# Turning two more x tiles in halves on two engines, and reordering the first products of v, in a fused attention and gated-MLP kernel

## The chip, the cores and the metric

The kernel runs on one core of a Trainium2 chip. The metric is the device time of one execution in microseconds (us), lower is better.

## The reference, cut to what matters

```python
xn = _layernorm(x)                              # x: 1 x 2048 x 512, bfloat16
return x + A(xn, wqkv, w_phi, wo) + B(xn, w_gate, w_up, w_down)
# A: qkv = xn @ wqkv; softmax features of q and k (32 heads of 16); kv = phi_k^T v; o = phi_q kv / den; o @ wo
# B: ((xn @ w_gate) * (xn @ w_up)) @ w_down     # 512 -> 1792 -> 512
```

Only the start matters here. Before TensorE can do useful work, the first four row tiles of x (128 x 512 each) must be loaded, have their row means removed ("centring"), and be transposed on TensorE ("turned"), since the products take it in that form. The division by the standard deviation is applied later, so it does not hold up the start. The product v(t) of a tile is four matmuls, one for each K-block of 128 rows of the v weights.

## The kernel before

TensorE's order is fixed by the program (`sc.pin = True`); every step waits by semaphore for what it reads. ScalarE is `act`, VectorE is `dve`.

```python
    load_x(0, 1)                 # loads, in the order of issue; SP and ACT are the two issuing queues
    load_x(1, 1, ACT)
    load_v(SP, 0)
    load_v(ACT, 1)
    load_x(2, 1)
    load_v(ACT, 3)
    load_v(SP, 2)
    load_x(3, 1)
    load_gu(SP, 0, (1,))         # first up weights
    ...
    load_gu(ACT, 0, (0,))        # first gate weights
```

```python
    def ln_mean_split(t):        # half the row mean on each of ScalarE and VectorE
        act(xn_tile(t)[:, 256:], x_tile(t)[:, 256:], ..., accum=mu[:, t:t + 1])
        dve(... xn_tile(t)[:, :256] ... accum_out=mua[:, t:t + 1] ...)
    def ln_mean(t):              # the whole mean on ScalarE
        act(xn_tile(t), x_tile(t), [("x", t)], [("mu", t)], scale=1.0 / 512.0, accum=mu[:, t:t + 1])
    def x_transpose(t, b, h=0, parts=1, eng=ACT):
        # 4 // parts transposes of 128x128 into PSUM bank b, then one copy ("turn") to SBUF by eng
```

```python
    x_transpose(0, 2, 0, 2)      # tiles 0 and 1: in halves; tile 1's copies on VectorE
    x_transpose(0, 3, 1, 2)
    warm(1, 128)
    x_transpose(1, 4, 0, 2, DVE)
    x_transpose(1, 5, 1, 2, DVE)
    warm(1, 128)
    ln_mean_split(2)
    ln_center_whole(2)
    ln_mean(3)
    ln_center(3)
    v_matmul(0, 0, (0,))         # K-blocks 0, 1 of v for tiles 0 and 1
    v_matmul(1, 1, (0,))
    v_matmul(0, 0, (1,))         # K-blocks 2, 3
    v_matmul(1, 1, (1,))
    x_transpose(2, 6)            # tile 2: whole, one copy on ScalarE
    for t in range(ND):
        ln_moments(t)            # row statistics, VectorE
    ...
    g0a()                        # first half of the first gate unit
    x_transpose(3, 7)            # tile 3: whole, one copy on ScalarE
    v_matmul(2, 2)
    v_keep(2, 2)
    u0a()                        # first half of the first up unit
    v_matmul(3, 3)
    v_keep(3, 3)
    g1a()                        # "the third gate group"
    ...
    w_fold(1, 0, 2)              # later: the first weight fold, used below as a mark
```

The eight `warm` matmuls of 512 columns ahead of this piece work on constants; they keep TensorE busy while the first loads are under way.

## Time and profile before

| | before |
|---|---|
| time, median of 3 runs (lowest, highest) | 214.45 us (214.41, 214.79) |
| span of the profiled execution | 212.6 us |
| TensorE busy | 207.7 us, 98% |
| x tile 3 landed | 7.26 us |
| first weight fold starts | 15.27 us |

The page of the kernel before: busy time by engine, and the chain of work that ended last.

```profile
span 212.6 us, 4025 instructions
...
PE 207.7 (98%) x1455; PEld 125.2 (59%) x1476; DVE 166.5 (78%) x277; ACT 144.6 (68%) x350; POOL 109.8 (52%) x137
...
PE 94%; DMA 2%; SPq 1%; issue 1%; DVE 0%; ACT 0%; DVEq 0%
```

TensorE (PE) is the bound. But the end of a matmul in this profile is modelled and overlaps the next one's start, so busy time hides short waits. The way to see them is the distance from one start to the next: it is 216, 109 or 56 ns for 512, 256 or 128 columns when nothing holds TensorE up, and anything above is a late start. One exception: a hole of exactly one more matmul (as the 432 ns, twice 216, before the start at 56.03 us in the kernel before) is taken for a record that the trace lacks, since other profiles have none at that place. The Trainium skill, "TensorE: Matmul & The Clock Gate", section "Wait — 56ns, not 53.3ns?", gives N / 2.4 GHz + 2.5 ns, which is 215.8 and 55.8 ns; this trace agrees.

The same chain in order of time, its first stretch: start, length, and what the time went to.

```profile
...
2.65 4.61 DMA arena<-in_A_x_dram
7.28 0.73 ACT arena L228 x2
8.11 0.36 DVE arena L451
8.52 0.40 PE ps L485 x4
8.92 1.95 PE ps L247 x11
10.87 0.05 issue
10.92 4.51 PE ps L247 x32
```

The load of x tile 3 lands at 7.26 us (2.65 + 4.61), ScalarE takes its mean (two instructions), VectorE centres it (L451), and only then do the transposes of tile 3 (L485) start, at 8.52. From there on TensorE waits no more.

### The profile page before, as it was taken

The page shows a single profiled execution, that of the slowest core. Times are in us where ns is not written, and L with a number is a line of the kernel's source. Part 1 is how long each engine was busy: PE and PEld are TensorE (multiplying, and loading weights), DVE is VectorE, ACT ScalarE, POOL GpSimd, SP SyncE. Part 2 cuts the span into 40 slices and gives each one's busy share as a digit, 9 for nine tenths or more (in the row PEclk, how much of TensorE's full clock was granted, in tenths as well). Part 3 has the DMA queues.
Part 4 walks back from the last instruction along what each step waited for, and adds up shares of the span by engine and source line. Part 5 has one row for each costly group of instructions (what it writes and reads, how often), then busy time and mean ns, then how long its engine had stood idle before and what let it go on. Part 6 is the DMA issues. An engine that isn't in the chain of part 4 may idle for free.

```text
span 212.6 us, 4025 instructions
## 1 busy us (share of the span) xinstructions
PE 207.7 (98%) x1455; PEld 125.2 (59%) x1476; DVE 166.5 (78%) x277; ACT 144.6 (68%) x350; POOL 109.8 (52%) x137
## 2 busy tenths in 40 slices
PE   8999999999999999999999999999999999999995
PEld 2575444444554444444444444556888898899884
DVE  4659999987995547568699988986888898898622
ACT  5588899985889999978778967564544444432220
POOL 4032464540330366998995882004559559558540
PEclk9999999999999999999999999999999999999999
DMA  5999990699100230331611340414265736637411
GB/s 172 299 300 376 162 175 6 80 343 196 25 3 0 35 63 3 52 67 33 88 40 23 71 80 0 119 53 51 49 79 125 172 78 152 141 85 175 123 49 49
DMA packets 49251, 22.29 MB, mean 105 GB/s; under 512 B 38096, under 2 KB 47696, under 8 KB 49232
## 3 DMA queue, kind: packets, MB, share of 16 engines
q1 hardware_dynamic: 48272, 21.39, 45.4%
q10 hardware_dynamic: 960, 0.66, 1.0%
q8 instruction: 11, 0.18, 0.4%
q14 instruction: 8, 0.07, 0.1%
HBM read 11.03 MB, written 2.10 MB: 62 GB/s over the span
## 4 chain that ended last, share of the span: by engine, by line
PE 94%; DMA 2%; SPq 1%; issue 1%; DVE 0%; ACT 0%; DVEq 0%
PE ps L247 89%; DMA arena<-in_A_x_dram 2%; PE ps L563 2%; PE ps L621 2%; PE ps L381 1%; SPq L292 0%; SPq L272 0%; ACT arena L228 0%; DVE arena L934 0%; PE ps L485 0%; DVE arena L451 0%; DVEq L1359 0%
## 5 line engine op out<-in xcount | busy, mean ns | idle before, releaser
L247 PE MATMUL ps<-arena 128*128 128x512 bf16 (+2 forms) x1139 | 197.8, 329 | 1.1
L247 PEld LDWEIGHTS ps<-arena 128*128 128x128 bf16 (+1 forms) x1160 | 110.6, 98 | 73.6 <-ACT arena L228 0.5
L228 ACT ACTIVATE arena<-ps 128x512 bf16<-128x512 f32 (+4 forms) x117 | 59.2, 541 | 11.2 <-PE ps L247 7.9
L228 ACT ACTIVATE arena<-arena 128x32 f32<-128x32 f32 (+9 forms) x131 | 53.1, 421 | 11.4 <-DVE arena L517 6.0
L904 DVE TENSOR_TENSOR arena<-ps,arena 128x512 f16<-128x512 f32 (+1 forms) x56 | 38.3, 683 | 13.3 <-PE ps L247 7.0
L527 POOL TENSOR_TENSOR arena<-arena 128x1024 bf16<-128x1024 bf16 x16 | 31.8, 1993 | 26.7 <-ACT arena L228 26.7
L517 DVE TENSOR_REDUCE arena<-arena 128x64 f32<-128x1024 bf16 x32 | 38.2, 1212 | 8.1 <-ACT arena L228 7.9
L228 ACT ACTIVATE arena<-ps,arena 128x512 bf16<-128x512 f32 (+1 forms) x55 | 35.6, 663 | 11.4 <-PE ps L247 11.0
L865 POOL TENSOR_TENSOR arena<-arena 128x256 f16<-128x256 f16 x32 | 23.8, 755 | 14.3 <-DMA arena<-arena 13.1
L843 DVE TENSOR_TENSOR arena<-arena 128x896 f16<-128x896 f16 x32 | 26.0, 811 | 3.4 <-PE ps L247 3.4
L228 ACT ACTIVATE ps<-ps 128x256 f32<-128x256 f32 x24 | 8.8, 368 | 29.0 <-PE ps L247 20.9
L934 DVE SCALAR_TENSOR_TENSOR arena<-ps,arena 128x256 bf16<-128x256 f32 (+1 forms) x24 | 13.2, 566 | 8.9 <-PE ps L247 8.8
L783 POOL TENSOR_TENSOR arena<-arena 128x512 f16<-128x512 bf16 x14 | 16.3, 1173 | 6.1 <-DVE arena L904 5.2
L969 POOL TENSOR_TENSOR arena<-arena 128x512 f32<-128x512 f32 x8 | 9.5, 1191 | 17.0 <-ACT arena L228 17.0
L533 POOL TENSOR_TENSOR arena<-arena 128x512 bf16<-128x512 bf16 x16 | 16.9, 1058 | 0.8
L631 DVE TENSOR_TENSOR arena<-ps,arena 128x512 f16<-128x512 f32 x16 | 11.0, 685 | 1.3 <-ACT arena L228 0.5
L531 POOL TENSOR_TENSOR arena<-arena 128x32 f32<-128x32 f32 x16 | 5.2, 324 | 10.4 <-ACT arena L228 5.9
L405 DVE BATCH_NORM_STATS2 arena<-arena 128x6 f32<-128x512 bf16 x16 | 10.4, 670 | 0.0
L463 POOL TENSOR_SCALAR arena<-arena 128x1 f32<-128x1 f32 x12 | 3.1, 274 | 12.9 <-ACT arena L228 12.9
L678 DVE BATCH_NORM_STATS2 arena<-arena 128x6 f32<-128x512 bf16 x14 | 8.9, 680 | 0.0
L563 PEld LDWEIGHTS ps<-arena 128*128 128x128 bf16 x128 | 6.1, 97 | 3.5
L621 PEld LDWEIGHTS ps<-arena 128*128 128x128 bf16 x128 | 6.2, 97 | 1.2
(55 smaller groups left out, 70.5 us busy)
## 6 DMA issues: line engine op xcount, KB each, us to landing
arena<-in_A_x_dram SPq DMA_DIRECT2D x8, 256.0 KB, 3.3
out_dram<-arena SPq DMA_DIRECT2D x15, 128.0 KB, 2.0
arena<-in_B_w_down_dram SPq DMA_DIRECT2D x1, 1792.0 KB, 9.1
arena<-in_A_x_dram SPq DMA_DIRECT2D x3, 512.0 KB, 4.3
arena<-arena SPq DMA_TRANSPOSE x44, 3.1
arena<-in_B_w_gate_dram SPq DMA_DIRECT2D x1, 640.0 KB, 8.5
arena<-in_B_w_up_dram SPq DMA_DIRECT2D x1, 640.0 KB, 9.6
arena<-in_B_w_gate_dram SPq DMA_DIRECT2D x1, 512.0 KB, 5.0
```

The source lines that it names most:

```text
L228: return sc.step(ACT, lambda e: e.activation(out=out_ap, in_=in_ap, func=func, scale=scale, **kw), reads, writes, 130.0 + 0.833 * n)
L247: ins = e.matmul(out_ap, lhsT=l, rhs=r, start=start and i == 0, stop=stop and i == npair - 1, **kw)
L517: dve(lambda e: e.tensor_reduce(out=sm, in_=e_v, axis=AX.X, op=ALU.add), [(name, s, 0), (name, s, 1)], [("sums", sr)], 1024)
L527: pool(lambda e: e.tensor_tensor(out=e_w, in0=e_w, in1=r_w, op=ALU.mult), [(name, s, 0), (name, s, 1), ("rs", n)], [(name, s, 0), (name, s ...
L533: pool(lambda e: e.tensor_tensor(out=e_v[:, :, 1, :], in0=e_v[:, :, 1, :], in1=rat[:, :, None].to_broadcast([128, H, 16]), op=ALU.mult), [ ...
L621: ins = e.matmul(bank(b0 + c // 4, (c % 4) * CW, CW), lhsT=ph[:, c, :], rhs=kvz_v[:, c, :], start=True, stop=True)
L631: dve(lambda e: e.tensor_tensor(out=o_tile(t).rearrange("p (b h f) -> p b h f", b=2, f=16), in0=nd[:, :, :, 0:16], in1=w_v[:, r].unsqueeze ...
L783: pool(lambda e, ft=ft: e.tensor_tensor(out=hH_v[:, ft, 0:512], in0=hT_v[:, ft, 0:512], in1=r2w, op=ALU.mult), [("hT", ft, 0), "r2w", ("x" ...
L843: dve(lambda e, k=k, i0=i0, i1=i1, op=op: e.tensor_tensor(out=s_block(p, k), in0=i0, in1=i1, op=op), ks + more, [s_key(p, k)] + over.get(k ...
L865: pool(lambda e, k=k, i0=i0, i1=i1, op=op: e.tensor_tensor(out=so_block(p, k), in0=i0, in1=i1, op=op), ks + [("so", p, m) for m in more], ...
L904: dve(lambda e: e.tensor_tensor(out=h_v[:, ft, sg * 512:(sg + 1) * 512], in0=bank(bu), in1=g, op=ALU.mult), [("ps", bu), ("g", s)] + ([("j ...
L934: dve(lambda e: e.scalar_tensor_tensor(out=o, in0=src, scalar=inv, in1=resid, op0=ALU.mult, op1=ALU.add), keys + [rkey, "inv"], [("ostg", ...
```

## The change

Its intent: give VectorE half of the turns of tiles 2 and 3 and half of the mean of tile 3, and put matmuls whose inputs are there ahead of those that wait. K-block 3 of v, loaded ahead of block 2, is used ahead of it; v(2) goes ahead of the first gate unit and of the transposes of tile 3.

```diff
+    x_transpose(0, 2, 0)
+    x_transpose(0, 3, 1)
     warm(1, 128)
+    x_transpose(1, 4, 0, DVE)
+    ln_mean_split(2)
+    x_transpose(1, 5, 1, DVE)
     warm(1, 128)
-    ln_mean_split(2)
     ln_center_whole(2)
-    ln_mean(3)
-    ln_center(3)
-    v_matmul(0, 0, (0,))
-    v_matmul(1, 1, (0,))
-    v_matmul(0, 0, (1,))
-    v_matmul(1, 1, (1,))
-    x_transpose(2, 6)
+    for t in range(2):
+        v_matmul(t, t, ((0, 1),), stop=False)
+    for t in range(2):
+        v_matmul(t, t, ((3,),), start=False, stop=False)
+    x_transpose(2, 6, 0)
+    x_transpose(2, 4, 1, DVE)
+    for t in range(2):
+        v_matmul(t, t, ((2,),), start=False)
+    ln_mean_split(3)
+    ln_center_whole(3)
+    (g0a, u0a, g0b, u0b), gate0 = up_unit(*ups.pop(0), pairs, 2)
+    (g1a, u1a, g1b, u1b), gate1 = up_unit(*ups.pop(0), pairs, 2)
+    v_matmul(2, 2)
+    x_transpose(3, 7, 0)
+    x_transpose(3, 6, 1, DVE)
+    v_keep(2, 2)
     for t in range(ND):
         ln_moments(t)
     ...
     g0a()
-    x_transpose(3, 7)
-    v_matmul(2, 2)
-    v_keep(2, 2)
     u0a()
```

(Helper functions lose the whole-tile case.)

More of the change, by code (lines that the diff above doesn't have):

```diff
@@ L401, in xk @@
     def xk(t):
-        return [("xnT", t, 0), ("xnT", t, 1)] if t < 2 else [("xnT", t)]
+        return [("xnT", t, 0), ("xnT", t, 1)] if t < ND else [("xnT", t)]
     def ln_moments(t):
@@ L441, in ln_center_whole @@
             [("x", t), ("mua", t), ("mu", t)], [("xn", t, 0)], 512, 0.27)
-    def ln_mean(t):
-        act(xn_tile(t), x_tile(t), [("x", t)], [("mu", t)], scale=1.0 / 512.0, accum=mu[:, t:t + 1])
-    def ln_center(t, parts=1):
-        n = 512 // parts
-        m, k = (mv_v[:, t, 0:1], ("mv", t)) if t % 2 == 0 else (mu[:, t:t + 1], ("mu", t))
-        for h in range(parts):
-            hs = slice(h * n, (h + 1) * n)
-            dve(lambda e, hs=hs: e.tensor_scalar(out=xn_tile(t)[:, hs], in0=x_tile(t)[:, hs], scalar1=m, scalar2=None,
-                                                 op0=ALU.subtract), [("x", t), k], [("xn", t, h)], n, 0.27)
     def ln_deferred():
@@ L475, in x_turn, with x_transpose @@
                turn=True)
-    def x_transpose(t, b, h=0, parts=1, eng=ACT):
-        n = NQ // parts
+    def x_transpose(t, b, h, eng=ACT):
+        n = NQ // 2
         qs = slice(h * n, (h + 1) * n)
@@ L486, in fn @@
             return ins
-        sc.step(PE, fn, [("xn", t, h), "ident"], [("ps", b)], n * 60.0)
+        sc.step(PE, fn, [("xn", t, h if t < 2 else 0), "ident"], [("ps", b)], n * 60.0)
         o = sb("xnT", 0, NQ * S_TOK).rearrange("p (q s) -> p q s", q=NQ)[:, qs, t * 128:(t + 1) * 128]
         i = bank16(b, 0, n * 128).rearrange("p (q s) -> p q s", q=n)
-        w = [("xnT", t, h)] if parts == 2 else [("xnT", t)]
+        w = [("xnT", t, h)]
         if eng == ACT:
@@ L538, in vs_tile, with v_matmul @@
         return sb("vs", (t % RK) * H * HC, H * HC).rearrange("p (h c) -> p h c", h=H)
-    def v_matmul(t, b, hs=(0, 1)):
-        for h in hs:
-            mm(bank(b), [(xnT(q, t * 128, 128), wv_v[:, q, :]) for q in (2 * h, 2 * h + 1)],
-               ([("xnT", t, h)] if t < 2 else [("xnT", t)]) + [("wv", 2 * h), ("wv", 2 * h + 1)], b, start=h == 0, stop=h == 1)
+    def v_matmul(t, b, qs=((0, 1), (2, 3)), start=True, stop=True):
+        for n, part in enumerate(qs):
+            mm(bank(b), [(xnT(q, t * 128, 128), wv_v[:, q, :]) for q in part],
+               ([("xnT", t, part[0] // 2)] if t < ND else [("xnT", t)]) + [("wv", q) for q in part], b,
+               start=start and n == 0, stop=stop and n == len(qs) - 1)
     def v_keep(t, b):
@@ L1022, in _build @@
     ln_center_split(1)
-    x_transpose(0, 2, 0, 2)
-    x_transpose(0, 3, 1, 2)
+    x_transpose(0, 2, 0)
+    x_transpose(0, 3, 1)
     warm(1, 128)
-    x_transpose(1, 4, 0, 2, DVE)
-    x_transpose(1, 5, 1, 2, DVE)
+    x_transpose(1, 4, 0, DVE)
+    ln_mean_split(2)
+    x_transpose(1, 5, 1, DVE)
     warm(1, 128)
-    ln_mean_split(2)
     ln_center_whole(2)
-    ln_mean(3)
-    ln_center(3)
-    v_matmul(0, 0, (0,))
-    v_matmul(1, 1, (0,))
-    v_matmul(0, 0, (1,))
-    v_matmul(1, 1, (1,))
-    x_transpose(2, 6)
+    for t in range(2):
[14 more added lines that the diff above has]
+    v_keep(2, 2)
     for t in range(ND):
         ln_moments(t)
-    (g0a, u0a, g0b, u0b), gate0 = up_unit(*ups.pop(0), pairs, 2)
-    (g1a, u1a, g1b, u1b), gate1 = up_unit(*ups.pop(0), pairs, 2)
     g0a()
-    x_transpose(3, 7)
-    v_matmul(2, 2)
-    v_keep(2, 2)
     u0a()
```

## The prediction

> **What bounds the kernel.** TensorE: the busy table gives it 207.7 of 212.6 us (98%), and the chain that ended last is 94% TensorE. In the timeline, matmul by matmul, starts follow each other every 216, 109 or 56 ns (512, 256, 128 columns). The Trainium skill, "TensorE: Matmul & The Clock Gate", "Wait — 56ns, not 53.3ns?", gives N / 2.4 GHz + 2.5 ns; the trace agrees. After 8.52 us no start is late, apart from holes of exactly one matmul (192 to 216 ns), which I take for missing records. So the change can only win before 8.52 us. From 5.49 us (first v product) on there are three real gaps: 0.17 us at 6.53 (third K-block of v, landed 6.43), 0.13 at 7.74 (first gate weights, landed 7.69), 0.33 at 8.52 (centring of tile 3, done 8.46). Sum 0.63 us, 0.3% of the time: the ceiling.
>
> **What the change does.** Same matrix work, another order; two more turns on VectorE, one more half mean.
> 1. K-block 3 of v (landed 5.60) goes ahead of block 2, which now follows the transposes of tile 2: removes the 0.17 us.
> 2. v(2) (4 x 0.216 us) goes ahead of the gate unit, so the gate starts near 8.7 us, after its weights: removes the 0.13 us.
> 3. Turns of tiles 2 and 3 split: a whole turn on ScalarE took 0.58 to 0.60 us, halves 0.38 (ScalarE) and 0.29 (VectorE) in parallel. v(2) needs this: only 0.43 us of products cover it.
> 4. Mean of tile 3 split: 0.42 + 0.19 us on ScalarE for 0.63 + 0.19 (0.1 to 0.2 less), but ScalarE first turns half of tile 2 (7.10 to 7.48), so the mean starts at about 7.40, not 7.28. Centring ends at about 8.42, hardly before 8.46, but v(2) now covers it instead of the short gate unit.
>
> **Estimate from those durations.** Block 3 of both tiles 6.35 to 6.79; transposes of tile 2 to 7.01; block 2 to 7.44; v(2) waits about 0.10 us for ScalarE's half turn and runs 7.54 to 8.40; transposes of tile 3 wait about 0.08 us; gate unit at 8.70; v(3) at 9.57, no wait; third gate group at 10.44, against 10.90 by summed cadences. Gain 0.45 us.
>
> **Afterwards.** All of it is on the critical path and should last, if nobody else becomes late. VectorE starts the row statistics at about 9.07, not 8.38, so rstd comes about 0.7 us later. By my count ScalarE has caught up by 18 us, 0.3 us before the first k features.
>
> **Prediction.** 214.45 - 0.45 = 214.0 us; 8 in 10: 213.7 to 214.45. Faster by over 2%: 0.01; within 2%: 0.98; slower: 0.01.
>
> **What the profile would show.** (1) no gap before block 3, none on a DMA before block 2; (2) no wait on gate weights; (3) v(2) starts at 7.5 to 7.6, released by ScalarE or VectorE; (4) transposes of tile 3 at 8.4 to 8.6, released by the centring; third gate group at about 10.45; no start late between 9 and 139 us; span about 212.15.
>
> **What would make it wrong.** Loads landing 0.2 us later or in another order; the half turns slower on both engines at once than alone; the VectorE order (copy, mean, copy, centring) delaying tile 2's centring beyond 6.7; late rstd stalling the first folds or features, which could give back all of it; a variation between runs (0.38 us here) as large as the gain.

## The result, and the profile after

| | before | after |
|---|---|---|
| time, median of 6 runs (lowest, highest) | 214.60 us (214.41, 214.85) | 214.44 us (213.88, 215.03) |
| ratio of means, 95% interval | | 0.9989 (0.9969 to 1.001) |
| span of the profiled execution | 212.6 us | 212.9 us |
| x tile 3 landed | 7.26 us | 7.41 us |
| first weight fold starts | 15.27 us | 15.15 us |
| late starts of TensorE from 50 to 62 us | none | 0.38 us |

A ratio is the mean time of one kernel's fast runs over the mean of the other's of the same rounds, so it is not quite the ratio of the medians in the table. The median lies in the forecast range, at its very upper end. The gain is 0.16 us by the medians and 0.23 by the means, a third to a half of what was forecast, but the interval reaches from about 0.7 us faster to 0.2 slower: these times alone rule out neither the forecast gain nor none. The profiled execution after is even longer than the one before. The times of the changed kernel spread over 1.15 us here, those of the kernel before over 0.44; that is no property of the kernels, since later the kernel before spread over 0.98 to 1.33 us (11 executions each).

The page of the changed kernel: the lines that answer to those of before.

```profile
span 212.9 us, 4028 instructions
...
PE 208.2 (98%) x1455; PEld 125.3 (59%) x1476; DVE 167.3 (79%) x281; ACT 143.8 (68%) x350; POOL 109.9 (52%) x137
...
PE 96%; DMA 1%; DVE 1%; issue 1%
```

Its chain in order of time, from the start.

```profile
...
0.79 2.60 DMA arena<-in_A_x_dram
3.41 0.56 DVE arena L427 x3
...
4.49 0.65 PE ps L474 x4
5.14 0.11 PE ps L1001
5.25 0.43 PE ps L474 x4
5.68 0.11 PE ps L1001
5.78 1.55 PE ps L247 x6
7.33 0.22 PE ps L474 x4
7.56 1.40 PE ps L247 x6
8.96 0.28 PE ps L474 x4
9.23 1.52 PE ps L247 x11
```

L427 are half means, L474 transposes, L1001 a warming matmul, L247 the products. The chain no longer goes through the load of tile 3. It starts with tile 0 (landed 3.39) and runs through TensorE from 4.49 us on. That was the aim. But the same matmuls now take longer than they should. First, the first product of v, before and then after, as the timeline shows it (start, duration).

```profile
5.49 0.38 PE L247 MATMUL ps<-arena 128*128 128x512 bf16 x1
```

```profile
5.58 0.63 PE L247 MATMUL ps<-arena 128*128 128x512 bf16 x1
```

0.63 us for a matmul that took 0.38: in the execution after, TensorE was still at half its rate. Start to start it took 427 ns, then 303 (part at half, part at full rate), then 216. Full rate came at about 5.3 us in the execution before and at about 6.2 in the one after. Up to 5.47 us both programs give TensorE the same instructions, so the change can hardly have caused this; the same program, run again below, reached full rate at about 5.65 us. The two late starts that came of it, 0.21 and 0.09 us, and some slow transposes ahead of them took most of the gain of the front.

Second, the stretch from 50 to 62 us. VectorE in the kernel before, two groups of its timeline, with the idle time ahead of them in brackets:

```profile
50.38 0.41 DVE L465 TENSOR_SCALAR arena<-arena 128x512 bf16<-128x512 bf16 x1 [1.36 <-DMA arena<-arena]
...
53.94 0.68 DVE L904 TENSOR_TENSOR arena<-ps,arena 128x512 bf16<-128x512 f32 x1
```

In the changed kernel, with TensorE's weight loads (PEld) that had to wait:

```profile
51.11 0.41 DVE L454 TENSOR_SCALAR arena<-arena 128x512 bf16<-128x512 bf16 x1 [2.20 <-DMA arena<-arena]
...
54.67 0.68 DVE L894 TENSOR_TENSOR arena<-ps,arena 128x512 bf16<-128x512 f32 x1
...
55.41 0.55 PEld L247 LDWEIGHTS ps<-arena 128*128 128x128 bf16 x4 [0.46 <-DVE arena L894]
...
58.37 0.55 PEld L247 LDWEIGHTS ps<-arena 128*128 128x128 bf16 x4 [0.47 <-DVE arena L894]
...
60.23 0.23 PEld L381 LDWEIGHTS ps<-arena 128*128 128x128 bf16 x4 [0.43 <-ACT arena L228]
```

VectorE normalises a later x tile (L465, L454) into a buffer that a transposing DMA must have read first. That DMA was 0.73 us later, so everything behind it in VectorE's queue was too, also the gate product (L904, L894) that frees a PSUM bank for TensorE. Three matmul starts, at 55.41, 58.38 and 60.24 us, were 0.13, 0.14 and 0.10 us late. The first two waited for that gate product, the third for ScalarE (L228), which had itself waited for VectorE until 54.79 us, again 0.73 later than in the kernel before. The busy time of the stretch doesn't show it, as the windows view of before and after says (columns: stretch, its length, then busy time of TensorE and so on):

```profile
50.00:62.00 12.00, 11.95 (x72) 5.86 (x72) 11.62 (x19) 8.92 (x21) 1.93 (x1) 1.00 0.24 47
```

```profile
50.00:62.00 12.00, 11.95 (x68) 5.28 (x67) 10.89 (x18) 8.09 (x18) 1.93 (x1) 1.00 0.28 56
```

TensorE is busy 11.95 of 12 us in both, with 0.38 us of late starts and without.

The transposing DMAs stand in SP's queue behind the loads of w_down and, right after it, wo. The DMA view of before and after (count, size, us from issue to landing):

```profile
arena<-in_B_w_down_dram SPq DMA_DIRECT2D x1, 1792.0 KB, 9.1
```

```profile
arena<-in_B_w_down_dram SPq DMA_DIRECT2D x1, 1792.0 KB, 10.1
```

It was issued 0.1 us earlier in the changed kernel (39.08, not 39.19) and still landed 0.85 us later. The load of wo behind it landed 0.72 us later (50.52, not 49.80), and the first transposing DMA behind both 0.73 later (51.01, not 50.28). In all eleven profiles that keep the two loads in this place, that DMA landed 0.47 to 0.56 us after the load of wo. So "slow w_down load" below stands for the two loads together.

### The profile page after: what moved, and what is told of

It is laid out like the page before. It is cut to its first block, busy times and chain, and to the rows that moved or that the text cites. A ratio compares the mean times of both kernels' runs of the same rounds, so it can differ in the third digit from the quotient of the medians.

```text
span 212.9 us, 4028 instructions
## 1 busy us (share of the span) xinstructions
PE 208.2 (98%) x1455; PEld 125.3 (59%) x1476; DVE 167.3 (79%) x281; ACT 143.8 (68%) x350; POOL 109.9 (52%) x137
## 4 chain that ended last, share of the span: by engine, by line
PE 96%; DMA 1%; DVE 1%; issue 1%
PE ps L247 91%; PE ps L611 2%; PE ps L553 2%; DMA arena<-in_A_x_dram 1%; PE ps L381 1%; PE ps L474 1%; DVE arena L427 0%; DVE arena L924 0%; DVE arena L434 0%; PE ps L1001 0%
## 5 line engine op out<-in xcount | busy, mean ns | idle before, releaser
L247 PE MATMUL ps<-arena 128*128 128x512 bf16 (+2 forms) x1139 | 198.4, 329 | 1.1
L247 PEld LDWEIGHTS ps<-arena 128*128 128x128 bf16 (+1 forms) x1160 | 110.7, 98 | 73.8 <-ACT arena L228 1.2
L228 ACT ACTIVATE arena<-ps 128x512 bf16<-128x512 f32 (+3 forms) x117 | 58.6, 539 | 12.9 <-PE ps L247 7.0
L228 ACT ACTIVATE arena<-arena 128x32 f32<-128x32 f32 (+9 forms) x131 | 52.9, 423 | 11.3 <-DVE arena L506 7.2
L894 DVE TENSOR_TENSOR arena<-ps,arena 128x512 f16<-128x512 f32 (+1 forms) x56 | 38.2, 683 | 11.8 <-PE ps L247 6.1
L228 ACT ACTIVATE arena<-ps,arena 128x512 bf16<-128x512 f32 (+1 forms) x55 | 35.9, 672 | 10.9 <-PE ps L247 10.4
L228 ACT ACTIVATE ps<-ps 128x256 f32<-128x256 f32 x24 | 8.8, 368 | 29.0 <-PE ps L247 27.0
L553 PEld LDWEIGHTS ps<-arena 128*128 128x128 bf16 x128 | 6.1, 97 | 3.5
L454 DVE TENSOR_SCALAR arena<-arena 128x512 bf16<-128x512 bf16 x12 | 5.4, 484 | 2.8 <-DMA arena<-arena 2.6
## 6 DMA issues: line engine op xcount, KB each, us to landing
arena<-in_B_w_down_dram SPq DMA_DIRECT2D x1, 1792.0 KB, 10.1
```

Source lines behind the costliest of these rows:

```text
L228: return sc.step(ACT, lambda e: e.activation(out=out_ap, in_=in_ap, func=func, scale=scale, **kw), reads, writes, 130.0 + 0.833 * n)
L247: ins = e.matmul(out_ap, lhsT=l, rhs=r, start=start and i == 0, stop=stop and i == npair - 1, **kw)
L894: dve(lambda e: e.tensor_tensor(out=h_v[:, ft, sg * 512:(sg + 1) * 512], in0=bank(bu), in1=g, op=ALU.mult), [("ps", bu), ("g", s)] + ([("j ...
```

## The experiments

**Theory 1.** The change works as forecast on the front, but two things that differ between executions of one program hid it in this profile: when TensorE's clock steps up, and how long loads take. The kernel before absorbs a late clock in its waits; the changed kernel has no waits left to absorb it. **Theory 2.** The change itself, by its later row statistics, causes the stall at 50 us.

Three columns below are read from traces. "Landing" is that of x tile 3; "fold" the start of the first weight fold, which all work of the front precedes; "late 50-62" the sum of late matmul starts in that stretch. Each kernel has 6 executions (one of them profiled). The means are of those. Runs 1 to 4, 5 to 8 and 9 to 12 in the table, without its first two rows, ran on three chips. Differences are taken from the nanoseconds of the trace.

| run | mean us | before | ratio, 95% interval | landing | fold | fold - landing | w_down load | late 50-62 |
|---|---|---|---|---|---|---|---|---|
| before (profile) | | | | 7.26 | 15.27 | 8.00 | 9.1 | 0 |
| after (first result) | 214.39 | 214.62 | 0.9989, 0.9969 to 1.001 | 7.41 | 15.15 | 7.74 | 10.1 | 0.38 |
| before_again | 214.71 | 214.71 | 1.0001, 0.9983 to 1.0019 | 7.53 | 15.54 | 8.00 | 9.0 | 0 |
| after_again | 214.31 | 214.71 | 0.9981, 0.9963 to 0.9999 | 7.57 | 15.01 | 7.45 | 8.2 | 0 |
| before_wd_early | 214.72 | 214.71 | 1.0001, 0.9985 to 1.0017 | 7.70 | 15.70 | 8.00 | 8.5 | 0 |
| after_wd_early | 214.23 | 214.71 | 0.9978, 0.996 to 0.9995 | 7.72 | 15.67 | 7.95 | 8.6 | 0 |
| before_x3late | 216.11 | 214.64 | 1.0068, 1.0048 to 1.0087 | 8.81 | 16.81 | 8.00 | 8.6 | 0 |
| after_x3late | 215.47 | 214.64 | 1.0038, 1.0016 to 1.006 | 8.55 | 15.97 | 7.43 | 10.1 | 0.42 |
| before_cold | 215.18 | 214.64 | 1.0017, 0.9996 to 1.0039 | 7.56 | 16.89 | 9.33 | 9.0 | 0 |
| after_cold | 215.22 | 214.64 | 1.0026, 1.0009 to 1.0043 | 8.21 | 16.26 | 8.05 | 7.9 | 0 |
| swap_only | 214.63 | 214.73 | 0.9995, 0.9973 to 1.0016 | 7.79 | 15.80 | 8.01 | 9.9 | 0.25 |
| no_swap | 214.51 | 214.73 | 0.9989, 0.9969 to 1.0009 | 7.38 | 15.74 | 8.36 | 8.5 | 0 |
| whole_turns | 214.51 | 214.73 | 0.9991, 0.9965 to 1.0018 | 7.49 | 15.22 | 7.73 | 9.4 | 0 |
| after_wg_later | 214.07 | 214.73 | 0.9969, 0.9948 to 0.999 | 6.57 | 14.90 | 8.33 | 8.1 | 0 |

All twelve runs gave correct results.

### The changed kernel again (after_again) and the kernel before again (before_again)

Edit: none in either.

> The changed kernel once more, unaltered. Marks: the first weight fold on TensorE (15.27 us in the profile before, 15.15 after, about 14.82 forecast) and the late matmul starts between 50 and 62 us (none before; 0.38 us after). Theory 1 (two things that differ between executions hid the gain: the step of the TensorE clock to full rate, near 5.3 us before and near 6.2 us after, and the landing of the w_down load, 48.3 us before and 49.2 after): this profile shows another clock step and another landing; a step near 5.3 gives a first fold near 14.8, and a landing near 48.3 gives no late start at 50 to 62; median of the timed runs 213.9 to 214.5, spread over 0.6 us. Theory 2 (the change itself makes the later row statistics stall VectorE at 50 to 60 us): 0.3 to 0.4 us of late starts there again, whatever the landing.

> The kernel before, unaltered, against itself: how far two timings of the same program differ. Theory 1: the gaps in front of 8.5 us shrink by as much as a late clock step costs, so the first fold stays within 0.15 us of 15.27 even if the step is late; times within 214.3 to 214.9; ratio 0.999 to 1.001. Theory 2 says nothing of it, save that no late start is seen between 50 and 62 us.

Measured: the changed kernel, once more, had a mean of 214.31 us, 0.40 below the kernel before. Its late starts in the front were two, 0.095 us (v(2) waiting for the half turns) and 0.042 (transposes of tile 3): forecast were 0.10 and 0.08. The clock was up by about 5.65 us, w_down took 8.2 us, and there was no late start at 50 to 62. The fold came at 15.01; near 14.8 had been expected for a clock step near 5.3. X tile 0 had landed 0.19 us later than in the profile of before (3.62, not 3.43), and everything up to the first product starts from that. From the first product of v to the fold it took 9.28 us (5.73 to 15.01), in the profile before 9.78 (5.49 to 15.27): counted from there, the gain is 0.50. VectorE's wait for the transposing DMA, which in the bad profile was 2.20 us:

```profile
49.89 0.41 DVE L454 TENSOR_SCALAR arena<-arena 128x512 bf16<-128x512 bf16 x1 [1.12 <-DMA arena<-arena]
```

The kernel before against itself gave 1.0001; one execution, 215.21, lay above the expected 214.9. In its own second profile the fold was 0.27 us later than in the first, not within 0.15 as expected. But tile 3 had landed 0.27 us later too, so the difference was again 8.00 us, although the clock stepped up later (about 5.6 us, as against 5.3).

Follows: theory 2 is refuted by after_again, which has the same late statistics and no stall: they do not suffice to cause it. And a rule shows: fold = landing of tile 3 + 8.00 us in the kernel before.

### Loads of w_down and wo moved out of the way (after_wd_early, before_wd_early)

```diff
         elif t == 3:
             load_qkT(0)
-        elif t == 5:
             load_w(SP, wd_v, ..., "wd", 1835008)
             load_w(SP, wo_v, ..., "wo", 524288)
```

> The changed kernel with the loads of w_down and wo issued right after the second transposed weight load (near 30 us, with the queue idle until 36 us), not in the middle of the turns of x near 39 us; the order of some ScalarE and VectorE work near 55 us moves with it. Theory 1: no late start of TensorE between 50 and 62 us in any profile, VectorE's wait for a turn of x (2.2 us in the profile after) goes below 0.5 us; times 0.1 to 0.3 us below those of the changed kernel, median near 213.9, no run over 214.6. Theory 2: the stall stays, since the row statistics are as late as before; times as the changed kernel's.

> The same move of the two loads in the kernel before. Theory 1: the kernel before has the same VectorE wait (1.4 us) with some slack left, so the move gains little, 0 to 0.2 us, median 214.3 to 214.6; the difference to the changed kernel with early loads is 0.3 to 0.5 us, the gain that was forecast. Theory 2: no effect, and the two kernels with early loads differ by 0.1 us or less, as the kernels themselves do.

Measured: in both profiles VectorE no longer waits for a transposing DMA between 44 and 62 us, and no matmul starts late there. The changed kernel gained 0.08 us in the mean over after_again (214.23, 214.31); one run, 214.72, was over the expected 214.6. The kernel before gained nothing (214.72, 214.71; its median, 214.69, is above the expected 214.3 to 214.6). Between the two kernels with early loads lie 0.49 us, in the expected 0.3 to 0.5. The profiled execution of after_wd_early was its slowest run: x tile 2 landed at 6.56 us and K-block 3 of v at 6.76 (5.42 and 5.60 in the profile before), and TensorE waited 0.82 us for these and what hangs on them.

Follows: the wait is removed by freeing the queue. The gain of it is too small for these runs to show; it can matter only to executions in which w_down is slow. The move also reorders some ScalarE and VectorE work near 55 us, so this run isn't proof by itself that the queue was the cause. swap_only below adds to it.

### Tile 3 on purpose late (before_x3late, after_x3late)

```diff
-    load_x(3, 1)
     load_gu(SP, 0, (1,))
+    load_x(3, 1)
```

> The kernel before with the load of x tile 3 issued after that of the first up weights. In three profiles of the kernel before (one with early w_down loads) the first weight fold came 8.00 us after the landing of x tile 3 (7.26 to 15.27, 7.53 to 15.54, 7.70 to 15.70). Theory 1, sharpened (the front of the kernel before is bound by that landing, through mean, centring, transposes and the matmuls after them; the change moves 0.58 us of matmuls ahead of that chain, so its whole gain shows only if nothing else binds the changed kernel): tile 3 lands 0.5 to 1.2 us later and the fold follows, again 8.00 us after it; time up by as much. Rival (the loads are a side matter, the gain is in shorter means and turns): fold less than 7.9 us after the landing.

> The same delay of tile 3 in the changed kernel, so that its landing binds here too. Theory 1: centring ends at landing + 1.1 us, transposes of tile 3 right after it, and the fold comes 7.42 us after the landing; so against the kernel before with the same late load the gain is 0.55 to 0.6 us, larger than between the two kernels themselves (0.2 to 0.4), and the spread of its times is no larger than that of the other. Rival: the gain is again 0.2 to 0.4 us or less.

Measured: the kernel before, fold minus landing, 8.00 us. The changed kernel, 7.43 us; expected were 8.00 and 7.42. Tile 3 landed 1.1 to 1.5 us later than in the three earlier profiles of the kernel before, a little more than the expected 0.5 to 1.2. The mean times differ by 0.63 us (216.11, 215.47), where 0.55 to 0.6 was expected, but with six runs each the 95% interval of this difference, worked out from the times, reaches about 0.65 us to either side, so it is the traces that carry this experiment. The profiled execution of the changed kernel lost 0.42 us again at 56 to 61 us with a w_down load of 10.1 us. The spread of the changed one, 1.43 us, was larger than the other's 1.16, where it should not have been larger; six runs each do not settle a spread.

The chain in order of time, before_x3late:

```profile
...
3.13 5.68 DMA arena<-in_A_x_dram
...
8.83 0.73 ACT arena L228 x2
...
9.66 0.36 DVE arena L451
...
10.07 0.40 PE ps L485 x4
10.46 1.95 PE ps L247 x11
```

and after_x3late:

```profile
...
3.12 5.42 DMA arena<-in_A_x_dram
...
8.57 0.52 ACT arena L228 x2
...
9.19 0.42 DVE arena L439
...
9.66 0.40 PE ps L474 x4
10.05 1.52 PE ps L247 x11
```

The first weight fold in the timeline, before_x3late and then after_x3late:

```profile
16.81 0.39 PE L381 MATMUL ps<-arena 128*128 128x128 bf16 x4
```

```profile
15.97 0.61 PE L381 MATMUL ps<-arena 128*128 128x128 bf16 x8
```

From landing to transposes it takes 1.26 us with a whole mean (8.81 to 10.07), 1.11 with the halved one (8.55 to 9.66): 0.15 us from the split. The rest, 0.43 us, is the v(2) (4 x 216 ns) that now goes ahead of the transposes, less the gate unit (4 x 109 ns) that now goes behind them. Sum: 0.58 us taken out of the chain behind tile 3, by the trace, when that chain binds both kernels.

### TensorE's clock late on purpose (before_cold, after_cold)

```diff
-    warm(7)
     warm(1, 512, [("x", 0)])
```

> The kernel before without seven of the eight warming matmuls of the start, so that TensorE's clock steps up late on purpose. Theory 1: starts at 427 ns for 512 columns until some time after 7 us; the gaps before 8.5 us are filled by the slower matmuls, so the cost is less than half of what a full stage at half rate would cost: fold 0.3 to 1.5 us later than 8.00 us after the landing of tile 3; time up 0.3 to 1.5 us. If the clock steps up as early as with the warming, the pair says nothing of theory 1.

> The changed kernel without the same seven warming matmuls. Theory 1: with the clock late, TensorE itself binds the front in both kernels, which hold the same matmuls, so the gain vanishes: within 0.15 us of the cold kernel before. Rival (the gain is independent of the clock): still 0.2 to 0.45 us faster than the cold kernel before.

Measured: means 215.18 and 215.22 us. By the means both lost to the late clock, the kernel before 0.54 us against its warmed self (the interval of its ratio just includes no loss), the changed one 0.91 against the 214.31 on another chip. The difference between the warmed kernels (0.23 and 0.40 us) is gone, as theory 1 expected; with intervals of about 0.2% on each ratio, a gain of some tenths cannot be excluded outright. The single profiles are no pair: the changed kernel's clock stepped up at about 8.3 us, the other's at about 10.0, so their folds (16.26, 16.89) compare executions, not kernels.

Follows: when TensorE itself is slow in the front, a change that only moves its work ahead of a wait has nothing to win. In before_cold the fold came 9.33 us after the landing: there the landing no longer binds. From 5.59 us until its clock stepped up, TensorE's matmuls follow each other at half rate with no wait between them.

### One part alone: the swap of the K-blocks (swap_only)

```diff
-    v_matmul(0, 0, (1,))
-    v_matmul(1, 1, (1,))
-    x_transpose(2, 6)
+    for t in range(2):
+        v_matmul(t, t, ((3,),), start=False, stop=False)
+    x_transpose(2, 6)
+    for t in range(2):
+        v_matmul(t, t, ((2,),), start=False)
```

> The kernel before with one part of the change: K-blocks 2 and 3 of v swapped, block 2 after the transposes of tile 2. Theory 1 (the front is bound by the landing of x tile 3 and what follows it): the wait for block 2 (0.17 us) goes, the wait before the transposes of tile 3 grows by as much, the first fold stays 8.00 us after the landing of tile 3, and the time is that of the kernel before within 0.1 us. Rival (each removed gap is a gain): 0.15 to 0.2 us faster.

Measured: no wait for block 2, and fold 8.01 us after the landing. The wait before the transposes of tile 3 was 0.19 us and did not grow, as was expected, from the 0.33 of the profile before: x tile 2 and block 3 landed late (6.66 and 6.85), and TensorE had already waited 0.44 and 0.35 us for them. Even these waits left the 8.01 as it was. Mean 214.63 as against 214.73: no gain beyond noise. And there is a stall at 58.9 and 60.8 us (0.25 us), with a w_down load of 9.9 us, in a kernel whose row statistics keep the place that they have in the kernel before. So the stall goes with the slow load and can come without the change. Over all fourteen profiles (the twelve runs, and the first ones of before and after), the three with a load of 9.9 us or more had the stall, the eleven with 9.4 or less did not (in three of these the loads had been moved out of the way). No run made the load slow on purpose, so the two are seen together three times, not tested as cause and effect. Nor is it shown that the change has no part in the size of the stall: it was 0.38 and 0.42 us in the changed kernel, 0.25 here. It could have one, since TensorE reaches this stretch sooner when the front is done sooner. In the three stalls the first held-up transposing DMA landed 35.7 to 35.9 us after the first fold, in the other eight with the loads in place 33.8 to 35.2.

### One part left out: no swap (no_swap), and whole turns (whole_turns)

```diff
     # no_swap
-        v_matmul(t, t, ((3,),), start=False, stop=False)
+        v_matmul(t, t, ((2, 3),), start=False)
     x_transpose(2, 6, 0)
     x_transpose(2, 4, 1, DVE)
-    for t in range(2):
-        v_matmul(t, t, ((2,),), start=False)
```

> The changed kernel without the swap: blocks 2 and 3 of v both ahead of the transposes of tile 2. Theory 1: the transposes of tile 2 now wait for block 2 of v as well (landed 6.3 to 6.7) and start at 7.4 to 7.6, v(2) at 8.1 to 8.3 in place of 7.55 to 7.9, and no spare matmuls cover its wait for the half turns (a gap of about 0.5 us); so most of the gain is gone: 0 to 0.15 us faster than the kernel before. Rival (the parts add up): 0.15 to 0.3 us faster.

```diff
     # whole_turns
-    x_transpose(2, 6, 0)
-    x_transpose(2, 4, 1, DVE)
+    x_transpose(2, 6, 0, ACT, 1)
     ...
-    x_transpose(3, 7, 0)
-    x_transpose(3, 6, 1, DVE)
+    x_transpose(3, 7, 0, ACT, 1)
```

> The changed kernel with whole turns of tiles 2 and 3 on ScalarE, as before. Theory 1: v(2) waits for a turn of 0.58 us in place of 0.38 and for all four transposes, so its gap grows from 0.10 to about 0.35 to 0.4 us; the mean of tile 3 on ScalarE starts 0.3 us later, so the transposes of tile 3 wait up to 0.1 us; the third gate group comes 0.25 to 0.35 us later: 0 to 0.15 us faster than the kernel before. Rival (the order of v(2) alone brings the gain): 0.3 us faster or more.

Measured: without the swap, v(2) waits 0.53 us for its half turns (about 0.5 expected). Its transposes of tile 2 and its v(2) started 0.2 us later than expected, at 7.76 and 8.51 us: tile 0 and block 2 landed late in this execution (3.73, 6.81). With whole turns, v(2) waits 0.42 us (0.35 to 0.4 expected) and the transposes of tile 3 0.04; those of tile 2 waited 0.17 for the centring of tile 2 as well. Both means are 214.51, 0.22 us below the kernel before, where 0 to 0.15 was expected. The waits came as theory 1 expects; the times can't tell 0.22 from 0.15, nor from the 0.23 and 0.40 of the whole change.

Follows, by the traces: the parts don't add up, they need one another. The swap alone wins nothing, but it provides the two matmuls that cover the turn of tile 2. The halved turns make this cover nearly long enough.

### A version for the new order (after_wg_later)

```diff
     load_x(3, 1)
-    load_gu(SP, 0, (1,))
+    load_gu(SP, 0, (0, 1))
     act(sbf("lnv", 0, 1), eps_f, ["eps"], ["pace"])
-    load_gu(ACT, 0, (0,))
```

on top of the early w_down loads.

> A version that might beat both: the changed kernel with early w_down and wo loads, and the first gate weights issued after x tile 3, since the gate unit now starts only at about 9 us. Theory 1: x tile 2, the v blocks and x tile 3 land 0.1 to 0.4 us earlier in the mean, as 256 KB no longer shares the queues with them; TensorE then waits only for the half turns and the centring (0.14 us, as in the best profile of the changed kernel) and, if the clock steps up late, for that; no new wait for gate weights at 9 us (landing before 8.6). Median 213.8 to 214.1, mean 0.1 to 0.3 us below the changed kernel's 214.31 of the earlier timing. If the landings do not move, the times are those of the changed kernel with early w_down loads (214.14).

Measured: tile 3 landed at 6.57 us, 0.7 to 1.2 us earlier than in the other profiles that kept its place in the queue, except after_cold, whose 8.21 was later still. The gate weights landed at 7.46. In the front only the two known waits were left, 0.097 and 0.042 us. Mean 214.07 and median 213.99, ratio 0.9969 to the kernel before, the largest gain and the only one besides after_wd_early and after_again whose interval stays below 1; the three intervals overlap. That it needs the change is not shown: the idea was that the gate weights may come later because the gate unit now starts near 9 us, but in this profile they landed at 7.46, ahead even of the 7.74 at which the kernel before starts its gate unit. The earlier landing of tile 3 is seen in one profile only. The timeline shows the fold:

```profile
14.90 0.61 PE L380 MATMUL ps<-arena 128*128 128x128 bf16 x8
```

Its mean is 0.66 us below that of the kernel before in the same call. What the later gate weights alone are worth is not measured.

## Why the prediction was right or wrong

- **Class and range: right, barely, and partly by luck.** The median of the first six runs, 214.44 us, is 0.01 below the upper end of the range, and these runs spread over 1.15 us. Over both timings (12 executions of the changed kernel; 23 of the one before, with before_again) the means are 214.35 and 214.69: a gain of 0.34 us where 0.45 was forecast. The 95% interval of this gain, worked out from these times, is about 0.1 to 0.6 us: there is a gain, and 0.45 is not ruled out.
- **The bound and the ceiling: right.** All the waits that the change could remove lay before 8.52 us.
- **The mechanism: right.** The swap, v(2) ahead of the gate unit, the halved turns and mean did what was said. The forecast waits of 0.10 and 0.08 us came as 0.095 and 0.041 in the first profile after, and 0.095 and 0.042 in the second. No gate weights were waited for. Late row statistics stalled nothing in after_again.
- **The step that did not hold: taking the sum of 0.45 us for the worth of the change,** "third gate group at 10.44, against 10.90". As a sum it was right: from the first product of v to the third gate group it means 4.95 us (from 5.49), and after_again took 4.93 (5.73 to 10.67), the profile before 5.43. But it laid both orders over the landings and the clock of one execution, in which the clock stepped up early, at 5.3 us. In the profile after it stepped up at 6.2: the third gate group came at 10.81, v(2) at 7.92 and not at 7.5 to 7.6, the transposes of tile 3 at 8.84 and not at 8.4 to 8.6, though each waited no longer than forecast. In before_again a step at about 5.6 us moved nothing, as fold and landing show: the waits before the transposes of tile 3 took it up. The worth of the change is thus not one number: it is 0.58 us when tile 3 binds both kernels (the late pair, by traces), and about zero when the clock binds both (the cold pair, by times, whose 95% interval reaches 0.6 us to either side).
- **"No start late between 9 and 139 us": wrong for the profiled execution.** There 0.38 us were lost at 55 to 60 us. The forecast looked for such a loss in the later row statistics; in the runs it goes with a slow w_down load ahead of the transposing DMAs, in the kernel before with the swap alone too; that the load causes it is supported by the early loads, which remove the wait, but not tested by a load made slow on purpose.
- **Two listed risks came true,** landings and a variation as large as the gain. The clock was not on the list, although the Trainium skill, "TensorE: Matmul & The Clock Gate", section "What's actually happening", says that the moment of the step is run-variable because its window is free-running. The twelve profiles with all the warming matmuls, the first of which started at 0.82 us in the profile before, agree: full rate came anywhere from before 4.6 us to 6.2.

What stays open: why one and the same w_down load takes 7.9 to 10.1 us, how often it is slow enough to stall, and whether the change makes the stall larger.

## What to carry to other kernels

When two marks differ by the same amount in every profile of a kernel, also when the first is delayed on purpose (here the fold, 8.00 us after the landing of one load, in all profiles with the warming matmuls), that load is what binds the stretch, and removing a wait elsewhere in it gains nothing. A change that removes waits also removes the slack that had absorbed variable things such as clock steps, as the traces show here (the times do not show that the changed kernel varies more). So forecast its gain for several executions, not for one, and look at several profiles before naming a cause. Once the order of use has changed, ask whether the order of loads still fits it; the version that did so had the lowest mean here, 214.07 us, though not clearly below the changed kernel's.

## What the Trainium skill lacked or had wrong

- "TensorE: Matmul & The Clock Gate", section "What's actually happening", speaks of about 3.4 us at half rate for a program's first matmuls. Here, with TensorE working from 0.82 us on, full rate came 3.8 us after that or earlier in some executions and 5.4 us after in another; without seven of the eight warming matmuls (the remaining one waits for x tile 0, landed 3.4 to 3.5 us) at about 8.3 us or about 10.0. The page advises against fitting a count of slow matmuls; it lacks that waits elsewhere can hide it, so that a tighter kernel pays for a step that its predecessor did not.
- "Perfetto Trace Analysis", section "Tensor Engine Instruction (MATMUL, LD_WEIGHTS)", says that a matmul's end is estimated, and the page elsewhere that matmul busy time is a poor measure. It lacks the consequence for short waits: in the stretch from 50 to 62 us busy time was 11.95 of 12.00 us with and without 0.38 us of late starts. Distances between starts show them.
- "DMA: Bandwidth & Descriptors", section "Latency and other measured facts", gives latencies but no spread of one load between executions. Here a 1,792 KB load took 7.9 to 10.1 us, and the 128 KB x tile 2, issued at 1.7 us, landed anywhere from 5.42 to 6.99.
